# Gaps of four floats between the rows that transfers move: a long convolution and a mixture of experts on one core

## The chip, the core and the metric

The kernel runs on 1 core of one Trainium2 chip. A core has five engines that run side by side: PE (TensorE) multiplies matrices, DVE (VectorE) and ACT (ScalarE) work on elements and empty PE's results, POOL (GpSimd) does element work and indirect transfers, and SP (SyncE) only issues transfers. The transfers run on 16 DMA engines between HBM and SBUF, the on-chip memory of 128 partitions. The metric is the device time of one execution in microseconds. The kernel before takes 1716.98 us, the median of three runs (1712.39 to 1722.12).

## The reference, cut to what matters

```python
def _attn_ref(x, v, pos_emb, w1, w2):          # B, S, D = 4, 11456, 128
    h_filt = (np.maximum(pos_emb @ w1, 0.0) @ w2) * window
    Uf = np.fft.rfft(x * v, n=2 * S, axis=1)
    Hf = np.fft.rfft(h_filt, n=2 * S, axis=0)
    y = np.fft.irfft(Uf * Hf[None, :, :], n=2 * S, axis=1)[:, :S, :]
    return x * y

def _moe_ref(x, w_skip, w_gate, w1, w2):       # x: 45824 x 128; w1: 8 x 128 x 1024
    out, on = x.copy(), x @ w_skip > 0
    xc = x[on]
    logits = xc @ w_gate
    e_idx, gate = argmax(logits), 1 / (sum(exp(logits - max)) + 1e-9)
    out[on] = xc + gate * (np.maximum(xc @ w1[e_idx], 0) @ w2[e_idx])
    return out
```

All values are float32. The first part is a causal convolution of x times v along the sequence with a filter that a small network makes from positions. The second sends each token whose skip score is positive through one of eight experts.

## The kernel before, in words

The convolution is done in blocks of 3840 positions, three blocks for each of 4 sequences, so 12 sequences of blocks (`NS`). The transform of 3840 points is split into 60 times 64. The channels are worked in four quarters of 32 (`DH`), so a row of one transform point holds 12 x 32 = 384 floats, 1536 B (`RUN`).

Stage one, `first_phase` (to about 150 us): class `First` loads x and v (`load`, line 191), multiplies them into `u` (`mult`, line 198; DVE in this stage, POOL later), transforms 60 points by a matmul (`data`, line 215), copies the result by ACT into `xs` (line 217) and stores it to HBM as `x1d` (`store`, line 203). One step is 4 of the 64 columns: two loads of 60 partitions, each with 6144 B of x and v in one row, and one store of 120 partitions with rows of 6144 B. There are 16 steps for each quarter. Between these steps the filter's network runs (`filt`, lines 227 to 292), fed by POOL's transfers of `post` (line 251).

The buffers of `First` are cut by `piece` out of `wf`, a tile of 16384 floats per partition that later holds the experts' weights: three of x and v (`xv`), two of their product (`us`), four of the transformed (`xs`), in all 12288 floats. What is left, `spare`, holds the first 32 of the 60 blocks of the constant `c2`; the other 28 lie in the tile `rest` (lines 335 to 349).

Stage two, `freq_phase` (to about 775 us): 60 steps, 15 for each quarter. A step loads 4 of the 60 points (`load`, lines 376 to 382, three steps ahead), transforms 64 points (line 392), combines it with the filter (lines 395 to 405, 412, 483, 484) and transforms back (line 423); ACT copies into `z` (line 424), and two transfers of 64 partitions store it to HBM as `zd` in rows of 1536 B (line 434). The steps of `First` for the next quarters are run in between. So the transfers `xv`, `x1d` and `zd` all go through SP's queue here, in the order in which the program issues them.

Stage three, `out_phase`: 32 chunks of 128 x 12 tokens. A chunk loads z with one transfer of 120 partitions with rows of 12288 B (`load_z`, line 1055; two buffers, issued when the last product of the chunk two before it is done) and three blocks of x (`ox`, line 1049, 128 partitions with rows of 2048 B), ends the transform by a matmul (line 1074), multiplies by x (DVE, line 1075), stores the rows (`out`, line 1079), computes scores and routes the tokens (lines 1083 to 1204). The steps of a chunk are sorted by lag and rank (lines 1275 to 1311) and issued in that order on every engine; between them, from about 893 us on, the experts' first batches of tokens are run (`early_slots`). What is left of the experts follows after about 1250 us (`late_slots`).

In the routing, `to` (line 1172, three sets of integer columns) and `no` (line 1200) are small tiles that DVE writes and reads.

Of the kernel before, what the change touches and what calls it, by code (L numbers as in the profile page):

```python
# [10 lines left out]
F32 = mybir.dt.float32  # L11
F32R = mybir.dt.float32r
F16 = mybir.dt.float16
I32 = mybir.dt.int32
# [8 lines left out]
K1, N2 = 60, 64  # L23
L = K1 * N2
H2 = N2 // 2
NS = NB * B
N = L * NS
NP = 4
DH = D // NP
# [5 lines left out]
PQ, PL = 49, 32  # L35
PP = PQ * PL // 2
OOB = 1 << 20
C, X, LP = H2 + 1, slice(64, 64 + E), 64

KNOWN = ((3, 4, 1), (5, 5, 1), (8, 8, 1), (13, 12, 1), (23, 12, 2), (29, 10, 2))  # L40
# [5 lines left out]
KS = 4  # L46
# [7 lines left out]
ZB = 2  # L54
# [97 lines left out]
class First:  # L152
# [4 lines left out]
    RUN = NS * DH  # L157
# [4 lines left out]
    def __init__(self, nc, i, x1d, x1f, mc, stage):  # L162
        self.nc, self.i, self.x1d, self.x1f = nc, i, x1d, x1f
        n = self.Q * self.RUN
        at = [0]

        def piece(k):
            at[0] += k * n
            return stage[:, at[0] - k * n:at[0]]
        self.xv = [piece(2).rearrange("n (a c) -> n a c", a=2) for _ in range(self.XV)]  # L170
        self.us = [piece(1) for _ in range(self.US)]
        self.xs = [piece(2)[0:2 * K1] for _ in range(self.XS)]
        self.used = at[0]

        for xv in self.xv:
            for rows in (slice(32, 64), slice(96, 128)):
                nc.vector.memset(xv[rows], 0.0)
        self.c1 = mc.tile([128, 2 * K1], F32, name="c1")
        nc.scalar.dma_start(self.c1, i["c1"])
        self.loaded, self.late = 0, []  # L180
# [25 lines left out]
    def data(self, step, pool):  # L206
        nc, Q, RUN = self.nc, self.Q, self.RUN
        h, ch = divmod(step, self.STEPS)
        u = self.us[step % self.US]
        xs = self.xs[step % self.XS].rearrange("k (m w) -> k m w", w=RUN)  # L210
        for q in range(Q):
            ps = [pool.tile([2 * K1, 512], F32, name="ps")[:, 0:RUN] for _ in range(2)]
            for p in range(2):
                rows = slice(p * 64, p * 64 + K1)
                nc.tensor.matmul(ps[p], self.c1[rows], u[rows, q * RUN:(q + 1) * RUN], start=True, stop=True)  # L215
            for p in range(2):
                nc.scalar.copy(xs[:, 2 * q + p], ps[p])  # L217
            if q == 0:
                self.store()
            if q < Q - 1:  # L220
                yield
        self.late.append((self.x1d[h][:, :, 2 * Q * ch:2 * Q * (ch + 1)].rearrange("k c m w -> (k c) m w"), xs))
        if ch == self.STEPS - 1:
            self.store()
        yield
# [100 lines left out]
def freq_phase(tc, nc, i, fi, zd, c3, spare, loads):  # L326
# [8 lines left out]
    HERE = spare.shape[1] // 128  # L335
    with (
# [10 lines left out]
        def c2(k, n=1):  # L347
            t, k = (spare, k) if k < HERE else (rest, k - HERE)
            return t[:, k * 128:(k + n) * 128]
# [22 lines left out]
        def load(n):  # L372
            h, k = divmod(n, PER)
            while done[0] < h * fi.STEPS * fi.Q:
                next(todo)
            ks = slice(KS * k, KS * k + KS)
            if h == 0:
                nc.sync.dma_start(c2(ks.start, KS), i["c2"][:, ks.start * 128:ks.stop * 128])
            x1 = qx.tile([128, KS, (NS + NB) * DH], F32, name="x1")
            w = NB * DH  # L380
            nc.sync.dma_start(x1[:, :, 0:fi.RUN], fi.x1d[h][ks].rearrange("k c n w -> (c n) k w"))
            nc.sync.dma_start(x1[:, :, fi.RUN:], fi.x1f[ks, :, :, h * w:(h + 1) * w].rearrange("k c n w -> (c n) k w"))
            return x1
# [55 lines left out]
        todo = others()  # L439
        ys = {}  # L440
        xs = {n: load(n) for n in range(QX - 1)}
        for _ in range(LEAD):
            next(todo)
# [10 lines left out]
        for n in range(ALL + LAG):  # L454
            back = backer(n - LAG, ys.pop(n - LAG)) if n >= LAG else lambda blk: None
            if n + QX - 1 < ALL:
                xs[n + QX - 1] = load(n + QX - 1)
# [31 lines left out]
class Experts:  # L489
# [7 lines left out]
    def __init__(self, tc, i, out, lists, mc, wf):  # L497
# [40 lines left out]
        self.ids = mc.tile([128, NKNOWN + NLAST, 2], I32, name="ids")  # L538
        nc.vector.memset(self.ids, OOB)
        self.spots, self.names = {}, {}  # L540
# [304 lines left out]
    def late_slots(self, pool, queue):  # L845
# [4 lines left out]
        with (  # L850
# [111 lines left out]
            with tc.For_i(NLAST, total, 1) as s:  # L962
# [6 lines left out]
                ids = mb.tile([128, 2], I32, name="ids")  # L969
                nc.vector.memset(ids, OOB)  # L970
                ps = mpt.tile([128, 2 * T], F32, name="mto")[:, 0:2]
# [33 lines left out]
def out_phase(tc, i, out, zd, ex, consts):  # L1005
# [3 lines left out]
    nc = tc.nc  # L1009
    NT = NS  # L1010
    NCH = H2
    with (
# [3 lines left out]
      with (  # L1016
# [23 lines left out]
        c4s, xms, zx, zts, lgs = {}, {}, {}, {}, {}  # L1040
# [10 lines left out]

        def load_z(ch):
            if ch < NCH:
                zts[ch] = ob.tile([2 * K1, 2 * NP, NS * DH], F32, name="zt", bufs=ZB)
                nc.sync.dma_start(zts[ch], zs[ch])

        def load(q, x=None):
# [107 lines left out]
        def route(ch):  # L1165

            oh = chunks.pop(ch)
            sel = ob.tile([128, E, NT], F32, name="sel", bufs=1)
            nc.vector.tensor_tensor(sel, rk.rearrange("p (e t) -> p e t", t=NT), oh, ALU.mult)
            rs = ob.tile([128, NT], F32, name="rs")  # L1170
            nc.vector.tensor_reduce(rs, sel.rearrange("p e t -> p t e"), axis=AX.X, op=ALU.add)
            to = ob.tile([128, 3, NT], I32, name="to")
            nc.vector.tensor_scalar(to[:, 0], rs, 1.0, None, ALU.add)
            nc.vector.tensor_scalar(to[:, 1], to[:, 0], 5, None, ALU.arith_shift_right)
            nc.vector.tensor_scalar(to[:, 2], to[:, 0], PL - 1, None, ALU.bitwise_and)
            tf = ob.tile([128, 2, NT], F16, name="tf")
            nc.vector.tensor_copy(tf, to[:, 1:])
            chunks[ch] = tf
# [18 lines left out]
        def write(ch):  # L1197
            chunks.pop(ch)
            pl = ob.tile([PQ, PL], I32, name="pl")
            no = ob.tile([PQ, PL], F32, name="no")  # L1200
            nc.vector.tensor_scalar(no, places, 0.0, float(OOB), ALU.is_equal, ALU.mult)
            nc.vector.scalar_tensor_tensor(pl, places, float(ch * 128 * NS - 1), no, ALU.add, ALU.add)
            nc.sync.dma_start(ex.lists[ch * PP:(ch + 1) * PP].rearrange("(q l) w -> q (l w)", l=PL // 2), pl)
            written.append(ch)
# [7 lines left out]
        for ch in range(ZB):  # L1212
            load_z(ch)
# [45 lines left out]
        def routed(ch):  # L1259
            route(ch)  # L1260
            last = ch == NCH - 1
            if last or ch in checks:
                counts = ob.tile([E * NS, C], F16, name="now")
                nc.vector.tensor_copy(counts, ex.counts)
                span = (NKNOWN, NTAB, 1) if last else checks[ch]
                tables.append(ex.table(counts, last, *span, ob, keep, tabs))

        def produced(ch, blk):
            product(ch, blk)
            if blk == NB - 1:  # L1270
                load_z(ch + ZB)
            load(NB * ch + blk + ZT - 1)
# [4 lines left out]
        for ch in range(NCH):  # L1277
            for blk in range(NB):
                for lag, rank, f in ((0, 0, produced), (1, 4, turn), (2, 4.9, score), (3, 2, score2), (STORE, 9, store)):
                    steps.setdefault(first(ch) + blk + lag, []).append((rank, f, (ch, blk)))  # L1280
            for lag, order, f in (
                    (6, 3, choose), (7, 1, exp), (7, 4.5, count), (7, 6, counted), (7, 6, gate), (8, 4.4, total),
                    (9, -2.5, even), (9, 0.5, spreadcounts), (9, 4.5, ranks),
                    (10, -2, routed), (11, 3, spread), (12, 4.5, collect), (13, -3, write)):
                steps.setdefault(first(ch) + lag, []).append((order, f, (ch,)))
# [106 lines left out]
```

## Time and profile before

The profiled execution took 1714.62 us, with a span of 1712.8 us.

| | |
|---|---|
| median of three runs | 1716.98 us (1712.39 to 1722.12) |
| profiled execution / its span | 1714.62 / 1712.8 us |
| PE busy | 1569.6 us (92% of the span) |
| DVE / ACT / POOL busy | 1203.0 / 830.2 / 1029.8 us |
| transfers | 353.73 MB in 182682 packets |
| SP's and ACT's data queue (q1), share of the 16 engines' span | 61.3% |
| mean granted clock of PE | 0.959 |

In the profile an engine's line number is that of the kernel's source. A tile in HBM or SBUF is named by its variable, or by the tile out of which it is cut: the x and v buffers, `xs` and `us` are all called `wf`, since they lie in it, and the loads of `x1d` into the second stage's tiles are called `x<-x1d`. In a row of waits stand the engine that was idle, the line of the instruction it waited to start, the engine and line that ended the wait, and then the time in all, the number of times and the longest. The DMA share is the time that packets took, over 16 engines; it can pass 1 where packets of two queues overlap on one engine.

### The profile page before, as it was taken

The page shows a single profiled execution, that of the slowest core. Times are in us where ns is not written, and L with a number is a line of the kernel's source. Part 1 is how long each engine was busy: PE and PEld are TensorE (multiplying, and loading weights), DVE is VectorE, ACT ScalarE, POOL GpSimd, SP SyncE. Part 2 cuts the span into 40 slices and gives each one's busy share as a digit, 9 for nine tenths or more (in the row PEclk, how much of TensorE's full clock was granted, in tenths as well). Part 3 has the DMA queues.
Part 4 walks back from the last instruction along what each step waited for, and adds up shares of the span by engine and source line. Part 5 has one row for each costly group of instructions (what it writes and reads, how often), then busy time and mean ns, then how long its engine had stood idle before and what let it go on. Part 6 is the DMA issues. An engine that isn't in the chain of part 4 may idle for free. (4 is left out here: it accounts for less than half of the span.)

```text
span 1712.8 us, 26697 instructions
## 1 busy us (share of the span) xinstructions
PE 1569.6 (92%) x8528; PEld 973.3 (57%) x8528; DVE 1203.0 (70%) x2529; ACT 830.2 (48%) x1740; POOL 1029.8 (60%) x679
## 2 busy tenths in 40 slices
PE   4885999999999999994679999999988999999996
PEld 1452333443434344441336777777677888888996
DVE  3221877777777789991477777768787777777985
ACT  2443455454554544431224555555454555555774
POOL 2101888888888878880014555523567777776884
PEclk9897999999999999996779999999999999999998
DMA  8699999999899988967888999988821111111110
GB/s 237 214 316 301 328 345 347 296 342 346 285 334 339 304 242 288 304 161 183 219 232 215 239 236 236 245 230 217 225 89 23 36 47 43 47 41 33 39 37 22
DMA packets 182682, 353.73 MB, mean 207 GB/s; under 512 B 55474, under 2 KB 127364, under 8 KB 178700
## 3 DMA queue, kind: packets, MB, share of 16 engines
q1 hardware_dynamic: 163452, 312.99, 61.3%
q0 software_dynamic: 18336, 38.67, 8.0%
q8 instruction: 69, 1.13, 0.3%
q14 instruction: 73, 0.60, 0.1%
q10 hardware_dynamic: 752, 0.34, 0.1%
HBM read 208.88 MB, written 144.02 MB: 206 GB/s over the span
## 5 line engine op out<-in xcount | busy, mean ns | idle before, releaser
L423 PE MATMUL zps<-y,c 128*128 128x512 f32 x720 | 337.2, 597 | 1.8 <-POOL y L483 1.4
L483 POOL TENSOR_TENSOR y<-y,p 128x2048 f32<-128x2048 f32 x60 | 271.6, 4527 | 82.5 <-DVE p L412 81.7
L767 POOL DMA_INDIRECT out<-o,ids x186 | 206.4, 1110 | 169.4 <-DVE o L773 122.9
L696 POOL DMA_INDIRECT xt<-out,ids x186 | 196.1, 1054 | 103.1 <-issue 47.6
L423 PEld LDWEIGHTS zps<-y,c 128*128 128x128 f32 x720 | 134.2, 190 | 171.3 <-issue 154.8
L412 DVE TENSOR_TENSOR p<-xp,g 128x1024 f32<-128x1024 f32 x240 | 217.4, 947 | 0.0
L412 DVE TENSOR_TENSOR y<-xp,g 128x1536 f32<-128x1536 f32 x120 | 210.7, 1756 | 4.1
L871 DVE SCALAR_TENSOR_TENSOR hh<-hp,hh 128x1024 fp32r<-128x1024 f32 x128 | 156.0, 1218 | 70.8 <-ACT hh L870 70.8
L662 POOL DMA_INDIRECT ids<-lists,at x93 | 106.8, 1148 | 151.7 <-DMA out<-xm 115.8
L424 ACT COPY z<-zps 128x512 f32<-128x512 f32 x180 | 105.6, 587 | 167.3 <-PE zps L423 165.0
L870 ACT ACTIVATE hh<-hp 128x1024 fp32r<-128x1024 f32 x128 | 132.2, 1033 | 74.5 <-PE hp L763 74.5
L1074 PE MATMUL y<-zt,c 120*64 120x512 f32 x384 | 116.9, 690 | 48.3 <-DVE xm L1075 22.8
L738 DVE TENSOR_TENSOR ws<-wf,ws 128x1024 fp32r<-128x1024 f32 x113 | 137.9, 1220 | 17.5 <-ACT ws L733 11.7
L215 PE MATMUL ps<-wf,c 60*120 60x384 f32 x512 | 123.4, 553 | 25.7 <-DVE wf L198 13.6
L484 POOL TENSOR_TENSOR y<-y,p 128x1024 f32<-128x1024 f32 x60 | 141.6, 2360 | 4.7
L1075 DVE TENSOR_TENSOR xm<-y,ox 128x512 f32<-128x512 f32 x96 | 66.2, 689 | 106.9 <-DMA ox<-xo 51.8
L217 ACT COPY wf<-ps 120x384 f32<-120x384 f32 x256 | 109.9, 485 | 57.7 <-PE ps L215 52.3
L392 PE MATMUL xp<-x,wf 128*128 128x480 f32 x256 | 122.7, 604 | 13.6 <-DMA x<-x1f 9.9
L404 DVE TENSOR_TENSOR g<-xp,g 128x128 f32<-128x128 f32 x120 | 34.7, 289 | 131.9 <-ACT g L397 131.8
L833 PEld LDWEIGHTS bank<-wd,h 128*128 128x128 f32 x928 | 107.8, 191 | 30.9 <-issue 30.8
L761 PE MATMUL hp<-hl,ws 128*128 128x512 f32 (+1 forms) x336 | 122.2, 364 | 2.3 <-DVE hh L871 0.9
L733 ACT CAST ws<-wf 128x1024 fp32r x113 | 117.9, 1043 | 6.7 <-issue 3.1
(191 smaller groups left out, 3180.1 us busy)
## 6 DMA issues: line engine op xcount, KB each, us to landing
wf<-xv SPq DMA_DIRECT2D x128, 360.0 KB
x1d<-wf SPq DMA_DIRECT2D x64, 720.0 KB
x<-x1d SPq DMA_DIRECT2D x60, 768.0 KB
zd<-z SPq DMA_DIRECT2D x120, 384.0 KB
zt<-zd SPq DMA_DIRECT2D x32, 1440.0 KB
out<-xm SPq DMA_DIRECT2D x96, 258.0 KB
ox<-xo SPq DMA_DIRECT2D x96, 256.0 KB
x1f<-fx POOLq DMA_DIRECT2D x16, 720.0 KB
```

The lines of the kernel that those rows point to most:

```text
L215: nc.tensor.matmul(ps[p], self.c1[rows], u[rows, q * RUN:(q + 1) * RUN], start=True, stop=True)
L392: nc.tensor.matmul(xp[:, k, 0:(NS + NB) * DH], c2(n % PER * KS + j * KH + k), x1[:, j * KH + k], start=True, stop=True)
L412: nc.vector.tensor_tensor(o[:, :, :, j * KH:(j + 1) * KH].rearrange("p s a k b d -> p (s a) k b d"), x[:, None].broadcast_to([128, m, KH, ...
L423: nc.tensor.matmul(zps, c3[:, a, :], y[:, blk, a], start=(a == 0), stop=(a == 1))
L483: nc.gpsimd.tensor_tensor(y[:, 1:], y[:, 1:], p1, ALU.add)
L484: nc.gpsimd.tensor_tensor(y[:, 2:], y[:, 2:], p2, ALU.add)
L696: ins = nc.gpsimd.indirect_dma_start(out=xt[:, j], out_offset=None, in_=self.rows[0:have], in_offset=bass.IndirectOffsetOnAxis(ap=ids[:, j ...
L738: eng.tensor_tensor(w[:, 1], src[:, ds(self.where(eng, tb), F)], w[:, 0].bitcast(F32), ALU.subtract)
L761: nc.tensor.matmul(hp, w[:, 0, c], hl[:, 0], start=True, stop=False)
L767: ins = nc.gpsimd.indirect_dma_start(out=self.rows, out_offset=bass.IndirectOffsetOnAxis(ap=ids[:, j:j + 1], axis=0), in_=o, in_offset=Non ...
L870: nc.scalar.activation(h[:, 0], hp, AF.Relu)
L871: nc.vector.scalar_tensor_tensor(h[:, 1], hp, 0.0, h[:, 0].bitcast(F32), ALU.max, ALU.subtract)
```

## The change

The rows that a transfer moves as one run in SBUF are set apart by `GAP`, four floats (16 B), which no transfer and no instruction touches.

- z: the tile `zt` has 8 rows of 388 floats instead of 384 in each partition. The transfer from HBM, whose source is still one run of 12288 B for each partition, goes to 8 rows of 1536 B.
- x and v: the buffer `xv` holds two rows of 772 floats instead of 768; the transfer goes to 2 rows of 3072 B instead of one of 6144 B.
- the stores of the first transform: `xs` holds 4 rows of 388 floats instead of 384; the transfer comes from 4 rows of 1536 B, and its destination in HBM is still one run of 6144 B for each partition. `us`, which no transfer touches, has no gap.
- The buffers of `First` take 12376 floats instead of 12288, so `spare` holds 31 blocks of `c2` instead of 32 and `rest` 29 instead of 28. The load of the four blocks 28 to 31 is cut in two where the tiles meet.
- The tiles `to` and `no` have one buffer instead of two, which makes room for the longer `zt`.

```diff
+GAP = 4
@@ class First, __init__
-        def piece(k):
-            at[0] += k * n
-            return stage[:, at[0] - k * n:at[0]]
-        self.xv = [piece(2).rearrange("n (a c) -> n a c", a=2) for _ in range(self.XV)]
-        self.us = [piece(1) for _ in range(self.US)]
-        self.xs = [piece(2)[0:2 * K1] for _ in range(self.XS)]
+        def rows(k, n, apart=GAP):
+
+            at[0] += k * (n + apart)
+            return stage[:, at[0] - k * (n + apart):at[0]].rearrange("p (a c) -> p a c", a=k)[:, :, 0:n]
+        self.xv = [rows(2, n) for _ in range(self.XV)]
+        self.us = [rows(1, n, 0)[:, 0] for _ in range(self.US)]
+        self.xs = [rows(2 * self.Q, self.RUN)[0:2 * K1] for _ in range(self.XS)]
@@ class First, data
-        xs = self.xs[step % self.XS].rearrange("k (m w) -> k m w", w=RUN)
+        xs = self.xs[step % self.XS]
@@ freq_phase, load
-                nc.sync.dma_start(c2(ks.start, KS), i["c2"][:, ks.start * 128:ks.stop * 128])
+                cut = min(max(ks.start, HERE), ks.stop)
+                for a, b in ((ks.start, cut), (cut, ks.stop)):
+                    if a < b:
+                        nc.sync.dma_start(c2(a, b - a), i["c2"][:, a * 128:b * 128])
@@ out_phase, load_z
-                zts[ch] = ob.tile([2 * K1, 2 * NP, NS * DH], F32, name="zt", bufs=ZB)
+                zts[ch] = ob.tile([2 * K1, 2 * NP, NS * DH + GAP], F32, name="zt", bufs=ZB)[:, :, 0:NS * DH]
@@ out_phase, route and write
-            to = ob.tile([128, 3, NT], I32, name="to")
+            to = ob.tile([128, 3, NT], I32, name="to", bufs=1)
-            no = ob.tile([PQ, PL], F32, name="no")
+            no = ob.tile([PQ, PL], F32, name="no", bufs=1)
```

## The prediction

> **What bounds the kernel now.** I read the page's DMA queues and issues first, then busy time by stretches, then the waits of the two stages in which transfers show, and last the DMA queues over short stretches in which one kind of transfer runs alone. All times are of the profiled execution, which took 1714.62 us, 1.84 beyond its span of 1712.8; it lies 2.4 under the median of the three timed runs, 1716.98, so what I find against it I move up by 2.4.
>
> The issues with the rows that change (KB of each transfer), then the stretches: busy us of the engines in order PE, weight loads, DVE, ACT, POOL, then granted clock, DMA share and GB/s.
>
> ```profile
> wf<-xv SPq DMA_DIRECT2D x128, 360.0 KB
> x1d<-wf SPq DMA_DIRECT2D x64, 720.0 KB
> zt<-zd SPq DMA_DIRECT2D x32, 1440.0 KB
> ...
> 43.00:86.00 43.00, 36.45 (x248) 19.98 (x246) 10.95 (x15) 20.14 (x42) 5.03 (x10) 0.88 0.70 216
> 200.00:300.00 100.00, 100.00 (x276) 39.37 (x275) 73.90 (x92) 51.70 (x129) 82.53 (x31) 1.00 1.02 346
> 300.00:400.00 100.00, 100.00 (x271) 40.09 (x269) 75.98 (x96) 49.54 (x125) 83.02 (x29) 1.00 0.98 322
> 400.00:500.00 100.00, 100.00 (x273) 40.12 (x270) 76.94 (x96) 50.18 (x127) 83.16 (x31) 1.00 0.97 315
> 500.00:600.00 100.00, 100.00 (x270) 40.01 (x269) 75.99 (x93) 50.17 (x126) 82.02 (x30) 1.00 1.00 325
> 905.00:1240.00 335.00, 326.31 (x2942) 239.69 (x2938) 251.31 (x925) 178.99 (x431) 163.29 (x148) 0.99 0.88 230
> 1240.00:1712.00 472.00, 447.77 (x2830) 391.60 (x2826) 358.77 (x695) 270.91 (x358) 340.38 (x313) 0.98 0.16 42
> ```
>
> From 200 to 600 PE is busy all the time, and the DMA engines are too (share 0.97 to 1.02): two limits that touch. From 905 on PE is busy 97% and then 95%; a faster transfer buys little there. Between, at the start of the output phase, neither holds. Three chunks of it, with the waits of PE and DVE from 743 to 905, and one chunk in order of time:
>
> ```profile
> 797.00:810.40 13.40, 7.38 (x52) 2.72 (x52) 2.08 (x3) 2.93 (x9) 0.00 (x0) 0.85 0.78 180
> 810.40:823.60 13.20, 8.28 (x53) 3.25 (x54) 4.85 (x16) 3.25 (x11) 0.00 (x0) 0.76 0.82 212
> 891.00:904.50 13.50, 9.68 (x81) 5.27 (x83) 8.78 (x36) 4.69 (x13) 3.93 (x4) 0.75 0.88 222
> ...
> PE y L1074 <- DVE xm L1075: 20.5, 7, 5.4
> PE y L1074 <- DMA zt<-zd: 17.6, 1, 17.6
> ...
> DVE xm L1075 <- DMA ox<-xo: 32.1, 8, 6.4
> ...
> 807.66 0.69 DVE L1075 TENSOR_TENSOR xm<-y,ox 128x512 f32<-128x512 f32 x1 [6.44 <-DMA ox<-xo]
> ...
> 810.42 0.34 SPq L1055 DMA_DIRECT2D zt<-zd  x1
> ...
> 810.86 0.81 SPq L1049 DMA_DIRECT2D ox<-xo  x2
> ...
> 820.87 0.69 DVE L1075 TENSOR_TENSOR xm<-y,ox 128x512 f32<-128x512 f32 x1 [5.92 <-DMA ox<-xo]
> ```
>
> Each chunk takes about 13.4 us, eight of them from 797 to 904.5. SP issues the 1440 KB of zt and 0.4 us later the ox that DVE needs next; the ox lies behind zt in the queue, DVE waits for it 32.1 us in eight times, and PE waits for DVE. So in this stage, and at the first zt (17.6 us), what zt takes is on the path. That is where this change can win.
>
> **The change part by part.** The z rows (32 transfers) become 8 pieces of 1536 B instead of one of 12288 B; the x and v rows (128) 2 of 3072 instead of one of 6144; the stores of x1d (64) 4 of 1536 instead of one of 6144. The bytes stay. The whole question is whether a short piece moves faster than a long row. Three stretches in which one kind runs alone: zt (783.3 to 789: 14 tiny packets and 98 of zt), the zd stores of 64 partitions in rows of 1536 B (761.8 to 764.9; SP issues nothing but these from 743.6 to 774), ox of 128 partitions in rows of 2048 B (778.7 to 779.4). A fourth, 27.0 to 27.6, holds rows of 6144 B, mostly of x1d.
>
> ```profile
> DMA packets 112, 1.20 MB, mean 211 GB/s; under 512 B 14, under 2 KB 14, under 8 KB 14
> q1 hardware_dynamic: 112, 1.20, 94.3%
> ...
> 743.63 30.91 SPq L434 DMA_DIRECT2D zd<-z  x10
> DMA packets 470, 0.69 MB, mean 222 GB/s; under 512 B 22, under 2 KB 470, under 8 KB 470
> q1 hardware_dynamic: 470, 0.69, 92.8%
> ...
> DMA packets 141, 0.26 MB, mean 370 GB/s; under 512 B 13, under 2 KB 16, under 8 KB 141
> q1 hardware_dynamic: 141, 0.26, 97.2%
> ...
> DMA packets 45, 0.21 MB, mean 348 GB/s; under 512 B 11, under 2 KB 11, under 8 KB 45
> q1 hardware_dynamic: 45, 0.21, 89.6%
> ```
>
> Time of one row = share x 16 engines x stretch / rows. zt: 0.943 x 16 x 5.7 / 98 = 0.88 us for 12288 B. zd: 0.928 x 16 x 3.1 / 448 = 0.103 us for 1536 B, and eight of them 0.82. ox: 0.972 x 16 x 0.7 / 128 = 0.085 us for 2048 B. So rows of 1536 B from 64 partitions run at 222 GB/s, hardly better than rows of 12288 B to 120 partitions at 211, and rows of 2048 B to all 128 at 370; rows of 6144 B reach 348. The rate goes with the partitions of the transfer, not with the length of its rows. A short row is no cure in itself.
>
> Sum for **z**: 1440 KB at 211 GB/s are 6.99 us. At the zd rate, 6.64: a gain of 0.35. At the ox rate, 3.99: a gain of 3.0. It counts nine times, for the first zt and for the eight chunks: 3 to 27 us. A loss on this transfer I bound by nothing in its rows but by the mid-stage rate below. I take the end near zd, since z keeps its 120 partitions, and round it to -1.
>
> [...]
>
> **x and v**: halves of 60 partitions, the case that is nearest to the zd stores; 0. In the first stage SP's transfers share the engines with POOL's "post", for which PE waits:
>
> ```profile
> PE fa L259 <- DMA post<-post: 6.4, 2, 6.2
> ...
> PE fa L259 <- DMA post<-post: 6.8, 3, 6.1
> ```
>
> Shorter pieces beside them may let post through sooner: between 0 and -13.2 us; no row shows the turn-taking of two queues, and I take -1.
>
> **Stores of x1d**: of 64, 16 belong to the first stage (share 0.70 in the stretch shown, there is room) and 48 to the middle one, 48 x 0.737 = 35.4 MB. Rows of 6144 B ran at 348 GB/s, 102 us for these; the middle stage with all its short rows at 346 at a share of 1.02, which is 339 at a share of 1 against 348 / 0.896 = 388: 14% more engine time, 104 instead of 91 us. Ends: 0 and +13 us of DMA time. It is hidden as long as the DMA engines keep ahead of PE; the room from 200 to 600 is about 0.02 + 0.03 of 100 us each, 5 us. I take +3.
>
> **SP**: more pieces per issue. Issue times (shortest/middle/longest ns):
>
> ```profile
> L1055 SPq DMA_DIRECT2D zt<-zd x32: 337/348/939, 778.6 to 1221.6; - x32
> L203 SPq DMA_DIRECT2D x1d<-wf x64: 322/346/1768, 22.4 to 617.6; - x64
> L381 SPq DMA_DIRECT2D x<-x1d x60: 379/526/2452, 156.5 to 728.2; - x60
> L382 SPq DMA_DIRECT2D x<-x1f x60: 371/1365/3280, 157.2 to 729.7; - x60
> L1201 DVE TENSOR_SCALAR no<-bank x32: 169/184/426, 839.0 to 1293.7; 49x32 f32<-49x32 f32 x32
> ```
>
> x<-x1d has 512 pieces and is itself issued in 0.38 at best, but the next issue after it (L382) takes 1.37 us in the middle: about 1 us for 512 pieces. zt with 960 would hold up the ox behind it by 2 us, hidden under the 4 to 7 us that zt occupies the engines; x1d with 480 holds up the next loads by 1, which are issued three steps ahead. 0.
>
> **The rest**: c2 no longer fits whole blocks into the spare part of wf (31 blocks instead of 32), one more issue of some 0.4 us among SP's gaps; 0. The tiles `to` and `no` lose their second buffer: DVE alone writes and reads both, in its own order; 0, and if a wait did arise, at most 32 x 0.18 = 6 us. PE and DVE read the same pieces as before at another step; 0.
>
> **Sum**: -1 (z) -1 (post) +3 (stores) = +1, against 1714.6, so 1715.6; moved up by 2.4: **1718 us**. The runs of the kernel before spread by 0.6%, so I call 0.5%, 8.6 us, what a measurement can tell from no change.
>
> **The rivals.**
>
> Faster: short pieces of z do get away from each other, and zt moves at the ox rate. Then 9 x 3.0 = 27 us go, since DVE is busy 8.8 of the 13.5 us of the last chunk and allows 10.4; 1714.6 - 27 + 2.4 = **1690**; half of it gives 1704. For it: the 0.88 us of a zt row is 1.7 times what 12288 B take at the ox rate (6 x 0.085 = 0.51), so there is something to be won, and the wait for ox would shrink at once. Against it: the zd row. [...]
>
> Slower: the middle stage tips over to the DMA engines. The 13 us of extra engine time for short stores fall in 400 us in which the share is already about 1; beyond 5 us of room each one is PE waiting for x (L392) and for POOL's product (L215). Price 13 - 5 = 8 with the room, 13 without: 1723 to **1730** with nothing gained elsewhere. For it: no idle engine time; SP is held up in issuing. Against it: PE waits for nothing there now, and loads run three steps ahead.
>
> The change doesn't do what it says: the side of the transfer that lies in HBM is one run, and if its length sets the packets, everything stays: **1717**. For it: the rows in HBM stay contiguous. Against it: no transfer of this kernel has gaps on one side alone, so no row speaks.
>
> **How the numbers follow.** The sum as it stands 0.40, packets as before 0.10, faster 0.31, slower 0.19. The likeliest is the sum, 1718, with its own range 1709 to 1726. The range over the cases is 1688 to 1732: it takes in both rivals' full price. The sum and the unchanged packets lie within 0.5%; the faster case is over 0.5% faster in nearly all its span, with a few hundredths from the sum's lower end; the slower one mostly over. So faster 0.32, same 0.48, slower 0.20.
>
> **What would show it.** Packets: under 2 KB in the stretch in which zt runs alone. If the GB/s there stays about 215 and the chunks between 797 and 905 at 13.4 us, the z step is right; 300 or more and chunks of 10 to 11 us prove the faster rival. Idle time before L423, L392 and L215 between 200 and 600, now zero, would prove the slower one. The waits of L259 for post tell that step. The prediction is wrong if zt moves clearly faster in short pieces from the same 120 partitions.

## The result and the profile after

The changed kernel takes **1726.97 us** (median of four runs, 1726.19 to 1729.01), the kernel before 1715.99 beside it (four runs, 1712.39 to 1722.12): ratio **1.0053, 95% interval 1.0029 to 1.0078**, 11 us slower. The profiled execution of the changed kernel took 1729.01 us, its span is 1727.2, 14.4 above that of before. In its lines, zt is issued at L1060, ox at L1054, the matmul y is L1079, the multiplication xm L1080, the first transform's matmul L217, `x1d`'s store L205, the load of x and v L193.

The transfers did what the change says. From the page after (packets of all queues, then SP's and ACT's data queue):

```profile
DMA packets 240426, 353.73 MB, mean 205 GB/s; under 512 B 55490, under 2 KB 189076, under 8 KB 240284
...
q1 hardware_dynamic: 221196, 312.99, 62.4%
```

Before there were 182682 packets; the bytes are the same. Where the 14.4 us lie is told by the starts of two groups of matmuls, the first product of the second stage and the matmul y of the output phase, before and after (shortest/middle/longest ns, then first to last start):

```profile
L392 PE MATMUL xp<-x,wf x256: 566/566/1140, 161.9 to 698.8; 128*128 128x480 f32 x128
L1074 PE MATMUL y<-zt,c x384: 592/643/1117, 790.0 to 1251.6; 120*64 120x512 f32 x192
```

```profile
L397 PE MATMUL xp<-x,wf x248: 566/566/1141, 160.2 to 696.4; 128*128 128x480 f32 x124
L1079 PE MATMUL y<-zt,c x384: 592/643/1117, 788.0 to 1264.4; 120*64 120x512 f32 x192
```

The second stage begins 1.7 us earlier, the output phase 2.0 earlier. Then all is lost: from the first y to the last it takes 476.4 us instead of 461.6, **14.8 more**. The stretches after (PE, weight loads, DVE, ACT, POOL, granted clock, DMA share, GB/s), the last two being two single chunks, from one issue of zt to the next:

```profile
43.00:86.00 43.00, 39.98 (x290) 21.95 (x288) 12.80 (x18) 22.68 (x47) 4.33 (x9) 0.96 0.86 260
200.00:300.00 100.00, 100.00 (x275) 39.29 (x274) 73.88 (x92) 51.41 (x128) 83.83 (x31) 1.00 1.03 340
300.00:400.00 100.00, 100.00 (x271) 40.05 (x270) 75.96 (x95) 49.95 (x126) 83.06 (x29) 1.00 0.99 320
400.00:500.00 100.00, 100.00 (x272) 39.83 (x270) 76.91 (x96) 49.81 (x125) 83.29 (x30) 1.00 0.99 323
500.00:600.00 100.00, 100.00 (x273) 40.05 (x272) 75.58 (x95) 50.37 (x126) 82.04 (x30) 1.00 1.02 325
905.00:1240.00 335.00, 318.24 (x2844) 233.00 (x2845) 242.94 (x895) 173.53 (x420) 154.79 (x144) 0.99 0.89 226
...
795.20:809.25 14.05, 7.59 (x52) 2.80 (x53) 2.08 (x3) 2.93 (x9) 0.00 (x0) 0.84 0.81 185
809.25:823.36 14.11, 8.08 (x53) 3.27 (x54) 4.84 (x16) 3.25 (x11) 0.00 (x0) 0.74 0.82 198
```

From 200 to 600 PE is busy all the time, as before, although the DMA share went up by 0.01 to 0.02 in each of the four stretches. From 43 to 86 PE is busier (39.98 us against 36.45). The chunks are 14.1 us long instead of 13.2 to 13.4. From 905 to 1240 PE was busy 8.1 us less.

The waits after, from 743 to 905 and then from 905 to 1240:

```profile
DVE xm L1080 <- DMA ox<-xo: 38.1, 8, 7.0
PE y L1079 <- DVE xm L1080: 26.6, 7, 6.8
PE y L1079 <- DMA zt<-zd: 17.2, 1, 17.2
...
DVE xm L1080 <- DMA ox<-xo: 43.5, 20, 4.5
PE y L1079 <- DVE xm L1080: 7.4, 10, 1.5
```

Before, the first three were 32.1, 20.5 and 17.6 us. For the second stretch the waits of before were:

```profile
DVE xm L1075 <- DMA ox<-xo: 19.8, 13, 2.5
...
PE y L1074 <- DVE xm L1075: 2.3, 5, 0.8
```

So the same wait as before, DVE for the ox behind zt, grew: by 6.0 us in the first stretch and by 23.7 in the second, where PE has other work and its wait for DVE grew by 5.1. (How long DVE waits there is no price by itself: in a kernel below, z2, it is 40.4 us and PE's wait 2.3 as before.) One chunk after, in order of time:

```profile
809.25 0.87 SPq L1060 DMA_DIRECT2D zt<-zd  x1
...
820.60 0.69 DVE L1080 TENSOR_TENSOR xm<-y,ox 128x512 f32<-128x512 f32 x1 [7.04 <-DMA ox<-xo]
...
823.36 0.87 SPq L1060 DMA_DIRECT2D zt<-zd  x1
```

This is a ring: zt is issued, the ox behind it arrives 11.35 us later, DVE multiplies, PE makes the chunk's last products, the buffer is free, the next zt is issued 2.76 us after the multiplication began. In the chunk shown of before the ox arrived 10.45 us after the issue of zt (810.42 to 820.87), and the next zt came 2.76 us after that, too. **The ring grew only between the issue of zt and the arrival of ox: by 0.90 us.**

Two things in that span changed. First the issue, for the three transfers (after; shortest/middle/longest ns); before, the load of x and v had a shortest of 322:

```profile
L1060 SPq DMA_DIRECT2D zt<-zd x32: 867/874/927, 777.0 to 1234.4; - x32
L193 SPq DMA_DIRECT2D wf<-xv x128: 842/1252/5402, 2.5 to 574.8; - x128
L205 SPq DMA_DIRECT2D x1d<-wf x64: 331/520/3657, 21.6 to 616.0; - x64
```

The middle issue of zt went from 348 to 874 ns, 0.53 us more. Second the flow: the stretch in which zt runs alone, from 783.3 to 789 as in the prediction.

```profile
DMA packets 760, 1.14 MB, mean 201 GB/s; under 512 B 16, under 2 KB 759, under 8 KB 760
...
q1 hardware_dynamic: 760, 1.14, 103.0%
```

201 GB/s instead of 211: 1440 KB take 7.34 us instead of 6.99, 0.35 more. The share passes 100% with one queue alone, so packets of one queue overlap too, not only those of two. One piece takes 1.03 x 16 x 5.7 / 743 = 0.126 us and eight 1.01 instead of 0.88, which is 15% more; as they overlap, 5% of it is left in the rate.

The two together are 0.88, and the ring grew by 0.90. But the time of the issue on SP isn't all that comes ahead of the data. In the two chunks shown the DMA engines are idle when zt is issued. Before and after, the stretch from the issue on in which nothing moves, and the 0.1 us behind it (last the DMA share and GB/s):

```profile
810.42:811.32 0.90, 0.90 (x4) 0.61 (x4) 0.85 (x3) 0.00 (x0) 0.00 (x0) 0.50 0.00 0
811.32:811.42 0.10, 0.10 (x5) 0.06 (x8) 0.10 (x1) 0.00 (x0) 0.00 (x0) 0.50 2.35 492
...
809.25:810.85 1.60, 1.60 (x14) 0.89 (x16) 1.49 (x5) 0.50 (x1) 0.00 (x0) 0.50 0.00 0
810.85:810.95 0.10, 0.10 (x2) 0.10 (x4) 0.10 (x1) 0.10 (x2) 0.00 (x0) 0.50 0.79 123
```

By the packets of the traces, zt's first data start 0.95 us after its issue before and 1.63 after (over the eight chunks 0.95 to 1.16 and 1.63 to 1.65). So of the 0.90 us by which this ring grew, 0.68 lie ahead of the first data and 0.22 behind it: the start of the transfer weighs more, and the flow less, than 0.53 and 0.35 say.

Over the 32 chunks: the third and the eleventh issue of zt, before and after.

```profile
796.97 0.34 SPq L1055 DMA_DIRECT2D zt<-zd  x1
...
907.55 0.39 SPq L1055 DMA_DIRECT2D zt<-zd  x1
```

```profile
795.20 0.88 SPq L1060 DMA_DIRECT2D zt<-zd  x1
...
912.80 0.87 SPq L1060 DMA_DIRECT2D zt<-zd  x1
```

These eight chunks took 110.58 us and now take 117.60, 7.0 more, 0.88 each. The 21 that follow, up to the last issue (1221.6 before, 1234.4 after), took 314.05 and now 321.60, 7.5 more. This measure, **eight chunks from the third issue of zt**, is used below for all runs.

### The profile page after: what moved, and what is told of

Its sections match the earlier page's. It is cut to its first block, busy times and chain, and to the rows that moved or that the text cites. A ratio compares the mean times of both kernels' runs of the same rounds, so it can differ in the third digit from the quotient of the medians.

```text
span 1727.2 us, 26699 instructions
## 1 busy us (share of the span) xinstructions
PE 1568.9 (91%) x8528; PEld 972.9 (56%) x8528; DVE 1201.7 (70%) x2529; ACT 830.2 (48%) x1740; POOL 1026.1 (59%) x679
## 5 line engine op out<-in xcount | busy, mean ns | idle before, releaser
L1079 PE MATMUL y<-zt,c 120*64 120x512 f32 x384 | 114.0, 674 | 63.9 <-DVE xm L1080 34.0
L1080 DVE TENSOR_TENSOR xm<-y,ox 128x512 f32<-128x512 f32 x96 | 66.2, 690 | 128.1 <-DMA ox<-xo 83.7
L217 PE MATMUL ps<-wf,c 60*120 60x384 f32 x512 | 125.7, 565 | 28.1 <-DVE wf L200 17.3
```

## The experiments

sp_extra, z2, z128_b and x128_z128 ran on a chip on which the kernel before takes 1717.36 us. The others ran on two on which it takes 1880.83 (only_z, no_z, z128, z128_gap) and 1884.26. Where z was left alone, as in no_z, the eight chunks agree with those of before on these chips too, and what differs lies behind: from 905 to 1000 the granted clock is 0.89 in no_z and 0.98 before. Each ratio is against the kernel before on the same chip, beside the run. All but no_z and its repeat, no_z_b, drop the gaps in x, v and the stores of `x1d`; `to` and `no` have one buffer throughout, which makes no difference to the eight chunks, as no_z shows.

**Which part costs: z alone, and all but z.**

```diff
 only_z: the kernel before, and
+    zts[ch] = ob.tile([2 * K1, 2 * NP, NS * DH + GAP], ...)[:, :, 0:NS * DH]
 no_z: the kernel after, and
-    zts[ch] = ob.tile([2 * K1, 2 * NP, NS * DH + GAP], ...)[:, :, 0:NS * DH]
+    zts[ch] = ob.tile([2 * K1, 2 * NP, NS * DH], ...)
```

> The kernel before with the gaps in z alone (and one buffer for the two small tiles). Theory P: the rate of a transfer goes with the partitions its engines reach at a time, so z in short pieces stays near 210 GB/s; what is lost is the longer issue on SP (0.87 us for 960 pieces where it was 0.35 for 120) and slightly slower pieces, some 0.5 us for each chunk of the output phase: about 12 to 15 us over the kernel before, 1727 to 1731. Rival M: the loss comes from the stores and loads of the first two stages, and z costs nothing: 1714 to 1719.

> The changed kernel without the gaps in z; x, v and the stores of the first transform keep theirs. Theory P: the output phase is as before (chunks of 13.4 us from 797 on), the first stage starts PE some us earlier but ends where it did: 1711 to 1717. Rival M: still 1724 to 1729.

only_z: 1899.26 us, ratio 1.0143 (1.0072 to 1.0214). no_z: 1875.75 us, ratio 1.0020 (0.9981 to 1.0060). The third and the eleventh zt of only_z, then of no_z:

```profile
797.36 0.85 SPq L1056 DMA_DIRECT2D zt<-zd  x1
...
914.26 0.86 SPq L1056 DMA_DIRECT2D zt<-zd  x1
```

```profile
796.51 0.34 SPq L1060 DMA_DIRECT2D zt<-zd  x1
...
906.33 0.34 SPq L1060 DMA_DIRECT2D zt<-zd  x1
```

116.90 us with z alone, 109.82 with all but z, against 117.60 and 110.58 of after and before. The loss is z's. Rival M isn't excluded by no_z's ratio alone, whose interval reaches 1.0060; it falls by the chunks and by the repeat below. only_z lost 18.4 us in the medians, more than theory P gave (12 to 15), and 6.3 in the eight chunks; the rest isn't explained. Its executions spread from 1881.66 to 1903.92 us, and the trace is of one of the two shortest, 1882.82.

The second of these, run again on another chip (no_z_b):

> The changed kernel with z in one row of 12288 B for each partition again; the gaps in x, v and the stores of x1d stay. Taken beside the others of this call. Nothing is left out. Theory Z (z is all of the loss; what the first stage gains in its waits for post is lost to other waits by 200 us, and PE hides the middle stage's stores): ratio 0.998 to 1.002, first product of the second stage 1 to 3 us earlier, y matmuls over 461 to 463 us as before. Rival S (short stores cost 13 us of DMA time that show somewhere): 1.004 to 1.008.

1876.16 us, ratio 0.9940 (0.9895 to 0.9985); eight chunks 110.78. So the rest of the change costs nothing that the two can find; whether it gains, as the second says and the first doesn't, stays open. The expected span of the y matmuls, 461 to 463 us, can't be read at the lower clock of these chips (535.8). The second stage's first product starts at 161.2 and 162.3 us in the two traces and at 161.9 before: the 1.7 us that the changed kernel had gained there do not return. Rival S, the price of short stores, falls, as the interval ends below 1.

**Is it the length of the rows or the partitions?** Two kernels load z into all 128 partitions; each chunk brings 8 rows of the next one that nobody reads. The one has rows of 12288 B, the other 8 pieces of 1536 B.

```diff
-        zs = zd.rearrange("m c k p h w -> m (c k) (p h) w")
+        zs = zd.rearrange("m c k p h w -> (m c k) (p h) w")
-                zts[ch] = ob.tile([2 * K1, 2 * NP, NS * DH], F32, name="zt", bufs=ZB)
-                nc.sync.dma_start(zts[ch], zs[ch])
+                zts[ch] = ob.tile([128, 2 * NP, NS * DH], F32, name="zt", bufs=ZB)
+                n, at = (128 if ch < NCH - 1 else 2 * K1), ch * 2 * K1
+                nc.sync.dma_start(zts[ch][0:n], zs[at:at + n])
...
 z128_gap: zt with rows of NS * DH + GAP, as in the change
```

> The kernel before, with z loaded into 128 partitions in the same long rows of 12288 B: 120 rows of the chunk and the first 8 of the next, which nothing reads (the last chunk takes 120). [...]

> The same with gaps of four floats: z into 128 partitions in pieces of 1536 B. Theory P: pieces run at 0.065 to 0.075 us each, so zt is 10% slower than with long rows, and SP's issue takes 0.9 us instead of 0.35; where chunks are set by transfers both show, 0.5 to 1 us for each of eight chunks: 4 to 10 us slower than the long rows in 128 partitions, still 15 us under the kernel before. [...]

> The kernel with z in long rows loaded into all 128 partitions (8 rows of the next chunk are loaded with each chunk and not used), taken beside the others of this call. Theory P (the rate goes with the partitions that the DMA engines reach at a time): zt runs at over 300 GB/s instead of 211, chunks between 797 and 905 us take 10 to 11.5 us instead of 13.4, and 15 to 25 us go in all, ratio 0.985 to 0.991. Theory L (the length of the rows sets the rate): 1.000 to 1.005.

z128: 1860.43 us, ratio 0.9906 (0.9865 to 0.9946). z128_gap: 1867.76, ratio 0.9961 (0.9923 to 1.0000). z128_b, the first kernel again on the faster chip: **1691.61 us, ratio 0.9854 (0.9832 to 0.9876)**. The stretch from 783.3 to 789, which also holds some ox, in z128 and in z128_gap:

```profile
DMA packets 217, 2.27 MB, mean 399 GB/s; under 512 B 22, under 2 KB 22, under 8 KB 34
...
q1 hardware_dynamic: 217, 2.27, 99.0%
```

```profile
DMA packets 1428, 2.17 MB, mean 381 GB/s; under 512 B 16, under 2 KB 1428, under 8 KB 1428
...
q1 hardware_dynamic: 1428, 2.17, 105.7%
```

399 GB/s with rows of 12288 B (379 in z128_b at a share of 91.1%): for zt the long rows were never slow, their 120 partitions were. With 128 the eight chunks take 89.43 us (88.47 in z128_b), 91.06 with gaps: 0.2 us more for each chunk, where 0.5 to 1 was expected; the issue is 0.53 us, not the 0.9 expected. Here too short pieces flow slower (381 against 399, one stretch each). At 120 partitions zt ran in this stretch at 201 GB/s with eight pieces (after), at 212 with two (z2, below), and at 211 and 212 with whole rows (before, and sp_extra below).

Is it how many rows are under way at a time? In the stretch the share is 94.3% before, which is 15.1 of 16, and 99.0% in z128, 15.8: 5% fewer before, not half. The packets of before's trace say the same: 15 rows of zt are under way for 4.80 of the 5.7 us, 16 or 17 for 0.89. By the lines shown, a row of 12288 B takes 0.88 us before and 0.49 in z128 (0.99 x 16 x 5.7 us, less 12 rows of ox, over 183 rows). So with 120 partitions nearly as many rows are under way at a time, and each takes 1.8 times as long; why it takes longer, no run here shows.

**Which half of z's loss is the issue, which the flow?** Two kernels, on the faster chip. sp_extra keeps z in long rows and has SP issue a small transfer ahead of each zt; z2 cuts each row once.

```diff
 sp_extra:
+                rest = ob.tile([128, E], F32, name="more", bufs=1)
+                nc.sync.dma_start(rest, i["rev"])
                 nc.sync.dma_start(zts[ch], zs[ch])
 z2:
+                zts[ch] = ob.tile([2 * K1, 2, NP * NS * DH + GAP], ...)[:, :, 0:NP * NS * DH]
+                nc.sync.dma_start(zts[ch], zs[ch].rearrange("r (p h) w -> r p (h w)", p=2))
```

> The kernel before, z in long rows, but ahead of each zt SP issues one more small transfer (128 rows of 32 B, 4 KB, into a tile that nothing reads). Nothing is left out. Theory I (what the short pieces cost is mostly the time in which SP issues zt, 0.87 us instead of 0.35, because SP issues zt at the moment its buffer comes free and the ox that DVE waits for stands behind it): one more issue of about 0.35 us ahead of each zt lengthens a chunk between 797 and 905 us by 0.3 to 0.4 us, and the whole by 5 to 11 us, ratio 1.003 to 1.006. Theory F (the pieces flow more slowly on the DMA engines, and the issue is hidden): 4 KB of data are nothing, ratio 0.998 to 1.002, chunks as before.

> The kernel before, with each z row in 2 pieces of 6144 B with one gap between them, instead of 8 pieces of 1536 B with eight gaps; x, v and the stores of x1d without gaps. Nothing is left out. Theory I: the issue of zt grows from 0.35 us to about 0.4 us only, and with it the loss: ratio 1.000 to 1.003. Theory F: pieces of 6144 B move at 0.45 us each, as half a long row; 1.000 to 1.002. Rival G (the gap itself, the changed place of the rows in SBUF, is what costs, not the number of pieces): 1.007 to 1.02, as with eight gaps.

sp_extra: 1721.19 us, ratio 1.0020 (1.0003 to 1.0037). z2: 1725.35 us, ratio 1.0037 (1.0021 to 1.0053). z2 missed what both theories expected. Its issues, the stretch of zt alone, and two issues of zt:

```profile
L1056 SPq DMA_DIRECT2D zt<-zd x32: 852/863/997, 777.2 to 1226.6; - x32
...
DMA packets 212, 1.21 MB, mean 212 GB/s; under 512 B 15, under 2 KB 15, under 8 KB 212
...
795.80 0.85 SPq L1056 DMA_DIRECT2D zt<-zd  x1
...
911.31 0.86 SPq L1056 DMA_DIRECT2D zt<-zd  x1
```

The error of the expectation is in the first line: I had taken the issue to grow with the pieces. It doesn't. One cut, 240 pieces, costs 0.863 us of SP, as much as 960 (0.874); the uncut one costs 0.348. The same step of 0.52 us stands in the shortest issue of the load of x and v (322 to 842 ns for one cut in each of 60 rows; the middle ones, 1286 and 1252, don't show it). Not every cut transfer pays it: the shortest issue of `x1d`'s store went from 322 to 331 ns only. What makes the step stays open. With 128 partitions it is smaller, 0.20 us:

```profile
L1057 SPq DMA_DIRECT2D zt<-zd x32: 523/528/997, 779.0 to 1280.6; - x32
```

So z2 splits the loss: the flow is as before (212 GB/s), the issue as after, and zt's first data start 1.62 to 1.64 us behind it, as after. Its eight chunks take 115.51 us, **+4.9 by the issue and the later start**; after has +7.0, so that **about 2 remain for the flow** (2.1, or 1.4 against only_z's 116.90; the three traces with whole rows, before and no_z twice, lie 1.0 apart). Each chunk: 0.62 and 0.26 us, where issue and rate alone gave 0.52 and 0.35, and start and rest 0.68 and 0.22. In the medians z2 loses 8.0 us and after 11.0. In the 21 chunks that follow z2 loses 1.2 us (315.3), sp_extra 3.5 and after 7.5; how that loss divides stays open. Rival G, the changed place in SBUF, isn't needed for the eight chunks. sp_extra shows that issue time ahead of zt is on the path by itself. The small transfer's issues:

```profile
L1056 SPq DMA_DIRECT2D more<-rev x32: 328/431/1280, 779.1 to 1227.4; - x32
```

Its eight chunks (798.19 to 911.04) take 112.85 us, 0.28 more each for an issue of 0.43, slightly less than expected; the ratio, too, lies below theory I's 1.003, at the upper end of theory F's. The chunks speak for theory I, the time alone doesn't decide.

**Is the ox behind zt the link?** Two kernels issue one ox of the next chunk ahead of zt.

```diff
-            if blk == NB - 1:
-                load_z(ch + ZB)
             load(NB * ch + blk + ZT - 1)
+            if blk == NB - 1:
+                load_z(ch + ZB)
 ox_first_z: the same in only_z
```

> The kernel before, z in long rows, but at the turn of a chunk the ox is issued ahead of zt instead of behind it, so that one of the three ox of a chunk passes zt in the queue. Nothing is left out. Theory I (a chunk is the time from the issue of zt to the arrival of the ox right behind it, then one multiplication by x and the last products): the stall is moved to the next ox and partly covered, chunks between 797 and 905 us take 11.5 to 13 us instead of 13.4, ratio 0.990 to 0.998. Rival F (the 1440 KB of zt and the ox fill the engines, whatever their order): 0.998 to 1.002.

> As above, ox ahead of zt, with z in 8 pieces of 1536 B with gaps (x, v and the stores without). Nothing is left out. Theory I (about half of what short pieces of z cost is the longer issue of zt, which holds up the ox behind it): against the run with ox first and long rows, the loss shrinks to the slower flow, 0.2 to 0.4 us for each chunk, 0.001 to 0.004 in the ratio. Theory F (the flow alone): the loss stays 0.005 or more, whatever stands behind zt.

ox_first: 1869.58 us, ratio **0.9924** (0.9889 to 0.9959). ox_first_z: 1873.33, ratio 0.9950 (0.9912 to 0.9988). Issues of zt in the one and the other:

```profile
796.85 0.34 SPq L1055 DMA_DIRECT2D zt<-zd  x1
...
893.40 0.34 SPq L1055 DMA_DIRECT2D zt<-zd  x1
```

```profile
797.69 0.85 SPq L1056 DMA_DIRECT2D zt<-zd  x1
...
896.63 0.86 SPq L1056 DMA_DIRECT2D zt<-zd  x1
```

96.55 and 98.94 us instead of 110.58 (109.82 and 110.78 in no_z on the same chip) and 116.90. One swapped pair of issues takes 1.75 us off each chunk, and DVE's wait for ox from 743 to 905 falls from 32.1 to 15.8 us, so the ring was what set the time, and rival F falls. With the ox ahead, short pieces of z cost 0.30 us for each chunk instead of 0.79: the issue of 0.86 us is nearly hidden then, the flow isn't. The two ratios differ by 0.0026, within what theory I gave, but their intervals overlap widely; the chunks carry this verdict.

**x and v in 128 partitions as well, and the swap on top.** x128_z128 has z in 128 partitions and loads x and v by one transfer of 128 partitions with rows of 6144 B (the host's layout holds four rows of zeros for each 60); x128_z128_ox has the swapped issues beside it.

```diff
-        for p in range(2):
-            self.nc.sync.dma_start(self.xv[step % self.XV][p * 64:p * 64 + K1], self.i["xv"][h, ch, p])
+        self.nc.sync.dma_start(self.xv[step % self.XV], self.i["xv"][h, ch])
```

> The kernel with z in 128 partitions as above, and x and v loaded by one transfer of all 128 partitions with rows of 6144 B instead of two of 60 partitions; the host's layout holds 4 rows of zeros more for each 60, and the two fills of the unused partitions with zeros at the start are dropped. Nothing else is left out. Theory P: x and v move at about 350 instead of some 215 GB/s and SP issues half as many loads; the first stage, in which PE waits for transfers, becomes 5 to 15 us shorter, 1 to 3 us less at the start; with z128 together ratio 0.975 to 0.987, below that of z128 alone. Rival (what x and v gain in the first stage is lost to PE's other limits by 200 us, as the lead of the shorter rows was lost): the ratio of z128 alone, within 0.003.

> The kernel with z, x and v in transfers of 128 partitions (rows that nobody uses are loaded with them), and ox issued ahead of zt. Nothing is left out. Theory P: the wait for ox, 13.1 us between 780 and 905 in that kernel, falls to under 6, and the time by 2 to 8 us below the 0.9814 of that kernel. Rival: with zt at 379 GB/s the ox is no longer what a chunk waits for, ratio 0.981 within 0.002.

x128_z128: **1686.08 us, ratio 0.9814 (0.9792 to 0.9837)**, beside z128_b's 0.9854. Its first product of the second stage and its last:

```profile
L388 PE MATMUL xp<-x,wf x256: 566/566/1140, 155.1 to 691.9; 128*128 128x480 f32 x128
```

6.8 us earlier than before (161.9), and the lead lasts through the middle stage (691.9 against 698.8). Of this about 5.5 us arrive in the medians, though the two intervals just touch. Whether a faster flow, half as many issues or the dropped fills bring the lead, no run separates. x128_z128_ox: 1843.63 us, ratio 0.9773 (0.9721 to 0.9825), on the slower chip; eight chunks take 81.38 us against 90.16 of x128_z128, and DVE waits 6.2 us for ox between 743 and 905 (expected: under 6; 13.1 before the swap). The two ratios come from different chips, and their intervals overlap: that the swap helps here is shown by the chunks, not by the times.

## Why the prediction was right or wrong

The measured 1726.97 lies in the range (1688 to 1732), but above the likeliest time, 1718, and just above that case's own range (1709 to 1726). It was 0.53% slower, with an interval that spans the 0.5% line on both sides. Of the three chances, "slower" had the least, 0.20. That the range holds the time is partly luck: its upper end is the slower rival's price of the middle stage, where nothing was lost.

- **What bounds the kernel.** Right, and the most useful part: the ox behind zt, in the output phase, is what the change touched, and the wait that grew. ox_first shows it by an experiment. The eight chunks are a little longer than was read: by the issues of zt they end at 907.55, not 904.5, 13.8 us each.
- **"The rate goes with the partitions, not with the length of its rows."** Right for the load of z, on which the forecast rests: 120 partitions stayed at 201 to 212 GB/s in one, two and eight pieces; 128 ran at 399 in long rows. The faster rival (1690) failed at the step that I had named against it, the zd row. As a rule for every transfer it isn't shown. The 348 GB/s were read as rows of `x1d`, but the loads of x and v have rows of 6144 B too and can't be told apart there. After the change the piece lengths tell them apart, and `x1d` leaves its 120 partitions at 192 GB/s from 56 to 58 us, alone, and at 359 from 29.5 to 30.5, where it is most of what moves:

```profile
DMA packets 250, 0.38 MB, mean 192 GB/s; under 512 B 0, under 2 KB 250, under 8 KB 250
...
DMA packets 221, 0.36 MB, mean 359 GB/s; under 512 B 4, under 2 KB 207, under 8 KB 221
```

- **The term of z, -1.** Mis-sized and of the wrong sign: it measured +14.8 us from the first y to the last. I had worked out only what a faster flow could win, and bounded a loss "by nothing in its rows but the mid-stage rate" without putting that bound into the sum; and the gain itself, 3 us at its lower end, was rounded to 1 without a reason. The bound, 339 against 388 GB/s, is 14% more engine time, 1 us for each zt; a piece did take 15% longer, and the rate lost 5%, 0.35 us. So the flow's loss lay inside a bound that I had and left out. The first zt, which I had counted as a ninth, lost nothing (PE waited 17.6 us for it and then 17.2).
- **The term of SP, 0.** This is the step that failed in its reasoning. I wrote that zt "would hold up the ox behind it by 2 us, hidden under the 4 to 7 us that zt occupies the engines". The cover doesn't exist, since the longer issue comes ahead of zt's own data: SP issues zt in the moment in which its buffer comes free, with nothing moving in the two chunks shown (DMA share 0.00), and the first data start 1.63 us after the issue instead of 0.95, so all that follows starts later. The size was wrong too: 0.53 us of SP and 0.68 until the data start, instead of 2, and set by the first cut, not by the 960 pieces. sp_extra and z2 price it: 0.28 us for a small issue, 0.62 for that of a cut zt.
- **"From 905 on PE is busy 97%; a faster transfer buys little there."** Not so for a slower one: 7.5 us of the loss lie in the 21 chunks behind the eleventh issue, at 912.8. An engine that is busy 97% isn't one that waits for nothing; its waits for DVE went from 2.3 to 7.4 us, and other groups moved with them.
- **post, -1.** The waits of PE for it, after:

```profile
PE fa L261 <- DMA post<-post: 5.5, 1, 5.5
...
PE fa L261 <- DMA post<-post: 3.0, 3, 2.5
```

  8.5 us instead of 13.2. But the second stage began only 1.7 us earlier, and in the two traces of no_z 0.7 earlier and 0.4 later. The sign of the term agrees with the first of these, and its size can't be told from their scatter; the wait for post isn't what sets the end of the first stage.
- **Stores, +3.** 0: PE is busy 100 of 100 us in all four stretches. The slower rival (1723 to 1730) got the time nearly right and the place wrong: not the middle stage, where PE has no idle time, but the output phase. The 14% of the term rests on the 348 GB/s that are not `x1d`'s alone.
- **The rest** (c2 in two parts, `to`, `no`, the reading at another step): 0, as taken; no_z holds all of it.

By steps, the sum of what was measured is -1.7 (first stage), -0.3 (middle stage, up to the first y), +14.8 (output phase) and +1.6 behind it: 14.4 of span, 11 in the medians.

## What to carry to other kernels

Where one engine issues a transfer at the moment its buffer comes free, and the next load that somebody waits for stands behind it, look for the issue on the path. Here it was (0.28 us for each chunk in sp_extra; 0.62 in z2, with the later start of the data): write down the ring (issue, arrival, multiplication, product, issue) and cost each link of it, before calling anything hidden. For the load of z the count of partitions decided, and the length of its rows hardly: 211 GB/s in 120 partitions and 399 in 128 with rows of 12288 B, 201 and 381 with pieces of 1536 B; filling up 120 to 128 with rows that nobody uses took 1.5% off this kernel. On another load that is worth a run before any work on its rows. And when two transfers leave at once, try issuing first the small one that is needed first: ox ahead of zt took 1.75 us off each of the eight chunks.

## What was not expected of the hardware

- One gap in the rows of zt, a load to 120 partitions, lengthens its issue by 0.52 us, and seven more add nothing: 348, 863 and 874 ns for 1, 2 and 8 pieces of a row. With 128 partitions 8 pieces cost 0.20 us (327 to 528). The first data of the 120-partition zt start 0.68 us later (0.95 to 1.63), more than the issue on SP grew.
- Pieces of 1536 B flow about 5% slower than rows of 12288 B at both rates (201 and 211 GB/s, 381 and 399); pieces of 6144 B don't (212). Why, no run here tells.
- z in 128 partitions moves 7% more bytes in 0.56 of the time, by the rates 211 and 399.
